# Weight rounding in a fused attention and feed-forward kernel: where a row's two words are added

## The chip, the cores and the metric

The kernel runs on one core of one Trainium2 chip. The metric is the device time of one execution in microseconds (us). The core has five engines, each with its own in-order instruction queue: PE (TensorE, the matrix products), DVE (VectorE), ACT (ScalarE), POOL (GpSimd) and SP (which here only issues transfers). They wait for each other through semaphores.

## The reference

Two blocks follow each other. The first is attention on q, k and v of shape (8, 12, 448, 64): q and k are normalised by their root mean square and a gain, then softmax(q k^T / 8) v. Its result, laid out as 3584 rows of 768, goes through a feed-forward layer:

```
def _moe_ref(x, w_in, w_out):
    h = x @ w_in            # 768 -> 2048
    r = np.maximum(h, 0.0)
    g = r * r
    return (g @ w_out).astype(np.float32)   # 2048 -> 768
```

q, k and v are 32-bit floats. The two weights come out of the set-up as 64-bit floats, since a 32-bit array is multiplied there by a 64-bit scalar. The kernel therefore reads each weight as two 32-bit words, a low and a high one that lie side by side, and makes a 32-bit float of them itself.

## The kernel before, in words

The work has these stages. The attention of the first two batch elements runs alone (`attention_alone`, twelve pairs of heads, about the first 133 us). Then comes the first product of the feed-forward layer for these (`first_product`, to about 262 us). From there on, the second product of one span of two batch elements is interleaved with the attention of the next, and so on through four spans; nothing of the change lies there.

Both products use a seven-product form of block multiplication. For it each weight is cut into blocks A11, A12, A21, A22 of 128 partitions by 384 words, and four sums of them are formed, S1 to S4. The seven operands A11, S2, S1, S3, A12, A22, S4 are stored to DRAM scratch (`w1s` for w_in, `w2s` for w_out) and read back in pieces (`sw`) as PE needs them, five pieces ahead.

The rounding is `prepare(t)`. There are 32 rows of 768 weights (`NFC` is 16, rows 0 to 15 belong to w_in, 16 to 31 to w_out), and each tick t has four quarters, between which the generator yields. An outer loop draws quarters: 48 of the first 52 over the attention alone, the others over the first product. The schedule is manual: on each engine the instructions stand in the order in which the program emits them. The steps of a row n are:

- `unsigned` (L578, ACT): the high words without sign, into an exponent buffer `eu`, one of four.
- L591 (DVE): clamps it. L596 (DVE): shifts it left by three; the result goes in place during the attention, and into a PSUM bank named `bits` from early in the first product on.
- L594 (ACT): scales the low words and makes integers of them.
- L601 (DVE): joins the sign bits of the high words to the shifted bits, into `eu`.
- `value` (L566, POOL), one tick later: the integer sum of low words and `eu` is the rounded weight. It is made in two instructions of 384 words, one for each block that the row fills. A row of w_in fills A11 and A12, or A21 and A22; a row of w_out A11 and A21, or A12 and A22.
- `total` (L572, POOL), after an odd row: S1, S2, S3, S4 of the pair of rows.
- the store of the seven blocks (L586, SP), three ticks after the odd row.

A pair of rows shares one of two block buffers in the tile `gC`, each of eight places: the seven operands in the order of the store, and A21 in place 7, which isn't stored. A new pair may be written into a buffer only once the store that reads it has landed. The words buffers, seven in turn, lie in `gC`, `gT` and a pool (`words`).

Other lines that are spoken of. In `attention_alone`, POOL takes the power -1/2 of a pair's mean squares (L702) and multiplies q by it (L704), behind the row sums (L699) and L700 on DVE; PE then transposes that pair (L742, tile `pt`), two pairs after its squares were taken. L767, L825 and L850 are PE's scores, values and sums of a pair; L784 on DVE adds up probabilities; L863 to L874 on DVE finish a pair, and L884 to L889 form sums of x for the first product. In `first_product`, seven products of 2.25 us (L1039, into banks `pa`, `pb`, `pc`, `pd`) make up one f of eight; DVE reads the banks: z (L1046), y (L1049), then g22, g21 and g12 (L1054), and ACT and POOL take it from there. pb, pc and pd share two banks in turn.

Of the kernel before, what the change touches and what calls it, by code (L numbers as in the profile page):

```python
# [9 lines left out]
F32 = mybir.dt.float32  # L10
U32 = mybir.dt.uint32
AF = mybir.ActivationFunctionType
ALU = mybir.AluOpType
# [373 lines left out]
def attention_then_ffn_bounded(  # L387
# [35 lines left out]
    nc = tc.nc  # L423
# [8 lines left out]
    NFC = DFF // P  # L432
# [47 lines left out]
    I32 = mybir.dt.int32  # L480
# [3 lines left out]
    NW = NPAIR * P  # L484
    HW = HC * P
# [7 lines left out]
    A11, S2, S1, S3, A12, A22, S4 = range(7)  # L493
    A21 = 7
# [3 lines left out]
    def pairs_of(words):  # L498
        both = words.rearrange("p (n two) -> p n two", two=2)
        return both[:, :, 0], both[:, :, 1]  # L500

    def words_of(n):
        place = n % WORDS
        if place == 0:
            at = BLOCKS * 8 * HW + EXPS * NW
            flat = stage[:, at:at + 2 * NW]
        elif place < 3:
            f = (NFC, HF)[place - 1] - 2
            flat = gT[:, f:f + 2, :].rearrange("p f n -> p (f n)")[:, 0:2 * NW]
        else:  # L510
            if (n, "words") not in spare:
                spare[n, "words"] = spare["pool"].tile([P, 2 * NW], F32, tag="words", name="words", bufs=WORDS - 3)
            flat = spare[n, "words"]
        return flat.bitcast(U32)

    def blocks_of(n):
        at = n // 2 % BLOCKS * 8 * HW
        return stage[:, at:at + 8 * HW].rearrange("p (k m) -> p k m", k=8)

    def exponents_of(n):  # L520
        at = BLOCKS * 8 * HW + n % EXPS * NW
        return stage[:, at:at + NW]
# [17 lines left out]
    def load_words(t, done):  # L540

        while loaded[0] <= t + WORDS - 3 and loaded[0] < max(done, 0) + WORDS:
            load_w(loaded[0])
            loaded[0] += 1

    def prepare(t):

        def there(n):  # L550
            return 0 <= n < 2 * NFC

        def parts(n):
            low, high = pairs_of(words_of(n))
            return exponents_of(n), exponents_of(n).bitcast(U32), low, high

        def value(n, half):
            if not there(n):
                return

            to = ((A11, A12), (A21, A22)) if n < NFC else ((A11, A21), (A12, A22))
            dst = blocks_of(n)[:, to[n % 2][half]]
            part = slice(half * HW, (half + 1) * HW)
            if doubles:
                _, eu, low, _ = parts(n)
                nc.gpsimd.tensor_tensor(*[x.bitcast(I32) for x in (dst, low[:, part], eu[:, part])], ALU.add)  # L566
            else:
                nc.gpsimd.tensor_copy(dst, words_of(n).bitcast(F32)[:, part])

        def total(n, dst, x, y, op):  # L570
            if there(n) and n % 2:
                nc.gpsimd.tensor_tensor(*[blocks_of(n)[:, i] for i in (dst, x, y)], op)  # L572

        def unsigned(n):

            if there(n) and doubles:
                e, _, _, high = parts(n)
                nc.scalar.activation(e, high.bitcast(F32), AF.Abs)  # L578

        if t == 0:  # L580
            unsigned(0)
        n = t - 3
        if there(n) and n % 2:
            c = n % NFC // 2
            dst = w1s[c] if n < NFC else w2s[:, c // 4, :, c % 4]
            nc.sync.dma_start(dst.rearrange("k p m -> p k m"), blocks_of(n)[:, 0:7])  # L586
            written[0] = n + 1
        if there(t) and doubles:
            e, eu, low, high = parts(t)

            nc.vector.tensor_scalar(e, e, 2.0 ** -15, 1.875 * 2.0 ** 16, ALU.max, ALU.min)  # L591
        yield
        if there(t) and doubles:
            nc.scalar.activation(low.bitcast(I32), low, AF.Copy, scale=2.0 ** -29)  # L594
            bits = banks.get("bits", eu)
            nc.vector.tensor_scalar(bits, eu, 3, 0x3FFFFFF8, ALU.logical_shift_left, ALU.bitwise_and)  # L596
        if t < 3:
            load_words(t, t - 1)
        yield
        if there(t) and doubles:  # L600
            nc.vector.scalar_tensor_tensor(eu, high, 0xC0000000, bits, ALU.bitwise_and, ALU.bitwise_or)  # L601
        total(t - 2, S3, A11, A21, ALU.subtract)
        total(t - 2, S4, A12, S2, ALU.subtract)
        value(t - 1, 0)
        yield
        unsigned(t + 1)
        value(t - 1, 1)
        total(t - 1, S1, A21, A22, ALU.add)
        total(t - 1, S2, S1, A11, ALU.subtract)
        load_words(t, t - 1)  # L610
        yield

    def ticks():
        for t in range(2 * NFC + 3):
            yield from prepare(t)
# [568 lines left out]
def kernel(  # L1184
# [50 lines left out]
    with tc.If(bits <= limit) as small_scores:  # L1235
        with tc.manual_schedule():
            attention_then_ffn_bounded(tc, *args, held)
# [32 lines left out]
```

## Time and profile before

| what | value |
|---|---|
| median of three runs | 1368.19 us (1366.46 to 1371.15) |
| profiled execution | 1369.76 us |
| its span, first to last instruction | 1367.8 us |
| granted TensorE clock in it | 0.998 |
| L566 on POOL | 64 instructions, 1.01 us each at the shortest |
| L572 on POOL | 64 instructions, 73.2 us |
| L601 on DVE | 32 instructions, 0.95 us each at the shortest |
| stores of a pair's blocks (L586) | 16, 1344 KB each, 5.7 to 10.3 us from issue to landing |

The profile's page gives the busy time of each engine and its share of the span, and the busy tenths of each engine in forty equal slices of 34 us. Groups name line, engine, operation, tiles (out<-in), shapes and count, then busy time and the mean of one in ns, then the idle time of the engine just before them with what ended it. An entry of the waits names who waited, then for whom. Busy time of PE overstates its work, since matrix products are pipelined; the idle time before its instructions is the better view of what it loses.

### The profile page before, as it was taken

The page shows a single profiled execution, that of the slowest core. Times are in us where ns is not written, and L with a number is a line of the kernel's source. Part 1 is how long each engine was busy: PE and PEld are TensorE (multiplying, and loading weights), DVE is VectorE, ACT ScalarE, POOL GpSimd, SP SyncE. Part 2 cuts the span into 40 slices and gives each one's busy share as a digit, 9 for nine tenths or more (in the row PEclk, how much of TensorE's full clock was granted, in tenths as well). Part 3 has the DMA queues.
Part 4 walks back from the last instruction along what each step waited for, and adds up shares of the span by engine and source line. Part 5 has one row for each costly group of instructions (what it writes and reads, how often), then busy time and mean ns, then how long its engine had stood idle before and what let it go on. Part 6 is the DMA issues. An engine that isn't in the chain of part 4 may idle for free.

```text
span 1367.8 us, 16894 instructions
## 1 busy us (share of the span) xinstructions
PE 1341.9 (98%) x5602; PEld 638.1 (47%) x5602; DVE 811.9 (59%) x1434; ACT 426.8 (31%) x657; POOL 633.2 (46%) x505
## 2 busy tenths in 40 slices
PE   8989999999999999999999999999999999999997
PEld 3333454444444455444444455444444445554553
DVE  6989776499986334467778523467788533332111
ACT  7875565433332011233332011233433101110000
POOL 6998887455563122555564122545666312220000
PEclk9999999999999999999999999999999999999999
DMA  9787998655675333446676433345765433333443
GB/s 245 194 234 198 329 390 291 184 117 118 133 141 126 97 86 87 102 113 136 130 140 121 111 93 87 100 110 106 157 124 114 99 91 89 90 90 101 106 114 66
DMA packets 434021, 190.12 MB, mean 139 GB/s; under 512 B 282885, under 2 KB 430725, under 8 KB 433925
## 3 DMA queue, kind: packets, MB, share of 16 engines
q1 hardware_dynamic: 425476, 180.10, 52.2%
q0 software_dynamic: 4736, 8.40, 2.4%
q8 instruction: 47, 0.77, 0.2%
q10 hardware_dynamic: 3712, 0.46, 0.2%
q14 instruction: 50, 0.40, 0.1%
HBM read 155.72 MB, written 33.16 MB: 138 GB/s over the span
## 4 chain that ended last, share of the span: by engine, by line
PE 86%; POOL 6%; DVE 4%; DMA 2%; issue 2%; ACT 1%; DVEq 0%; POOLq 0%; ACTq 0%
PE ps L1086 35%; PE pa L1039 10%; PE pd L1039 10%; PE pc L1039 10%; PE sc L759 7%; PE pav L836 6%; PE pb L1039 5%; POOL rstd L702 2%; POOL gC L566 1%; POOL gC L572 1%; DMA xT<-factors 1%; POOL qk L704 1%; DMA sw<-w1s 1%; ACT gT L771 0%; PE tot L850 0%
## 5 line engine op out<-in xcount | busy, mean ns | idle before, releaser
L1086 PE MATMUL ps<-gT,sw 128*128 128x448 f32 x768 | 301.1, 545 | 4.7 <-DVE p L1105 4.0
L1016 POOL TENSOR_TENSOR gT<-gT 128x448 f32<-128x448 f32 x96 | 93.9, 980 | 290.6 <-ACT gT L1012 290.6
L1086 PE MATMUL ps<-gC,sw 128*128 128x448 f32 x576 | 225.2, 542 | 0.0
L1086 PEld LDWEIGHTS ps<-gT,sw 128*128 128x128 f32 x768 | 144.4, 191 | 156.3 <-issue 145.6
L724 POOL TENSOR_TENSOR half<-half,mhalf 128x28 f32<-128x28 f32 x36 | 174.5, 4847 | 75.3 <-DVE half L723 72.1
L1086 PEld LDWEIGHTS ps<-gC,sw 128*128 128x128 f32 x576 | 108.0, 190 | 113.0 <-issue 110.1
L1039 PE MATMUL pa<-xT,sw 128*128 128x448 f32 x384 | 154.9, 539 | 0.0
L1012 ACT ACTIVATE gT<-gT 128x448 f32<-128x448 f32 x96 | 55.4, 577 | 311.6 <-DVE gT L1054 311.5
L761 ACT ACTIVATE pr<-sc 128x896 f32<-128x896 f32 x87 | 77.4, 915 | 121.5 <-PE sc L759 121.5
L759 PE MATMUL sc<-qkT 64*64 64x448 f32 (+1 forms) x1152 | 109.7, 496 | 0.0
L1039 PEld LDWEIGHTS pa<-xT,sw 128*128 128x128 f32 x384 | 72.9, 190 | 71.7 <-issue 70.3
L804 POOL DMA_DIRECT2D xT<-factors x72 | 38.0, 532 | 90.1 <-DMA factors<-square 61.0
L1054 DVE TENSOR_TENSOR gT<-z,pd 128x448 f32<-128x448 f32 x32 | 19.8, 620 | 99.7 <-PE pd L1039 99.6
L1039 PE MATMUL pb<-xC,sw 128*128 128x448 f32 x192 | 77.6, 540 | 1.4 <-issue 1.4
L1039 PE MATMUL pc<-xT,sw 128*128 128x448 f32 x192 | 77.5, 540 | 0.5 <-DMA sw<-w1s 0.5
L1039 PE MATMUL pd<-xT,sw 128*128 128x448 f32 x192 | 77.8, 541 | 0.0
L1039 PE MATMUL pc<-xC,sw 128*128 128x448 f32 x192 | 77.5, 540 | 0.0
L1039 PE MATMUL pd<-xC,sw 128*128 128x448 f32 x192 | 77.4, 539 | 0.0
L726 POOL TENSOR_TENSOR qk<-qk,half 128x448 f32<-128x448 f32 x72 | 75.0, 1061 | 2.8
L572 POOL TENSOR_TENSOR gC<-gC 128x384 f32<-128x384 f32 x64 | 73.2, 1162 | 2.5
L836 PE MATMUL pav<-pr,vt 64*64 64x448 f32 x348 | 72.7, 537 | 1.5 <-DVE half L872 1.5
L836 PE MATMUL rest<-pr,vt 64*64 64x448 f32 x348 | 72.7, 537 | 0.0
(135 smaller groups left out, 1879.7 us busy)
## 6 DMA issues: line engine op xcount, KB each, us to landing
sw<-w1s SPq DMA_DIRECT2D x224, 192.0 KB, 2.4
sw<-w2s SPq DMA_DIRECT2D x168, 256.0 KB, 3.2
w1s<-gC SPq DMA_DIRECT2D x8, 1344.0 KB, 7.5
w2s<-gC SPq DMA_DIRECT2D x8, 1344.0 KB, 8.1
out_dram<-osb SPq DMA_DIRECT2D x184, 56.0 KB, 1.9
qk<-in_q_dram SPq DMA_DIRECT2D x144, 56.0 KB, 3.6
qk<-in_k_dram SPq DMA_DIRECT2D x144, 56.0 KB, 2.9
xT<-factors POOLq DMA_DIRECT2D x72, 112.0 KB, 3.4
```

The lines of the kernel that those rows point to most:

```text
L572: nc.gpsimd.tensor_tensor(*[blocks_of(n)[:, i] for i in (dst, x, y)], op)
L702: nc.gpsimd.tensor_tensor(flat, flat, mhalf[:SP, 0:4 * NJ], ALU.pow)
L724: nc.gpsimd.tensor_tensor(half, half, mhalf, ALU.pow)
L726: nc.gpsimd.tensor_tensor(qkn[:, s], raw[:, s], half[:, s * NG:(s + 1) * NG].rearrange("p g -> p g ()").to_broadcast([P, NG, 32]), ALU.mult)
L759: nc.tensor.matmul(sc[part, h, 0:n], qkT[rows, 0, 1, keys], qkT[rows, 0, 0, of], start=True, stop=True)
L761: nc.scalar.activation(pr, sc[:, :, 0:n], AF.Exp)
L804: nc.gpsimd.dma_start(xT[h * D:(h + 1) * D, b % 2, hp], sums["out"][i % 2].rearrange("(h g) t -> h () (g t)", h=2)[h].to_broadcast([D, S]))
L836: nc.tensor.matmul(into, vs[i][rows, h, c, :], probs[i, c][rows, h, :], start=(c == 0), stop=(c == NF), skip_group_check=True)
L1012: nc.scalar.activation(g, src, AF.Relu)
L1016: nc.gpsimd.tensor_tensor(g, g, g, ALU.mult)
L1039: nc.tensor.matmul(ps, stream[n + i][:, c], rhs[:, c], start=first and c == 0, stop=c == HC - 1, skip_group_check=not first)
L1086: nc.tensor.matmul(ps, stream[n][:, c % 4], rhs_of[i][:, c], start=c == 0, stop=c == HF - 1)
```

## The change

The two POOL instructions of `value` become one DVE instruction for the whole row of 768 words. So that one access pattern can name the row's two blocks in rising order, a new function `place_of` puts the blocks of w_in rows at other places of the buffer: A21 at 0 and the seven operands at 1 to 7. The blocks of w_out rows stay where they were. The sums and the store use the same function. The call stands where that of the first half stood, behind L601 of the following row; the call of the second half, in the last quarter of the tick, goes. The branch for 32-bit weights is not taken here.

```diff
+    def place_of(n, k):
+
+        return 7 * int(n >= NFC) if k == A21 else k + int(n < NFC)
...
-        def value(n, half):
+        def value(n):
             if not there(n):
                 return
 
             to = ((A11, A12), (A21, A22)) if n < NFC else ((A11, A21), (A12, A22))
-            dst = blocks_of(n)[:, to[n % 2][half]]
-            part = slice(half * HW, (half + 1) * HW)
+            a, b = (place_of(n, k) for k in to[n % 2])
+            dst = blocks_of(n)[:, a:b + 1:b - a]
             if doubles:
                 _, eu, low, _ = parts(n)
-                nc.gpsimd.tensor_tensor(*[x.bitcast(I32) for x in (dst, low[:, part], eu[:, part])], ALU.add)
+                low, eu = (x.rearrange("p (h m) -> p h m", h=2) for x in (low, eu))
+                nc.vector.tensor_tensor(*[x.bitcast(I32) for x in (dst, low, eu)], ALU.add)
...
         def total(n, dst, x, y, op):
             if there(n) and n % 2:
-                nc.gpsimd.tensor_tensor(*[blocks_of(n)[:, i] for i in (dst, x, y)], op)
+                nc.gpsimd.tensor_tensor(*[blocks_of(n)[:, place_of(n, i)] for i in (dst, x, y)], op)
...
-            nc.sync.dma_start(dst.rearrange("k p m -> p k m"), blocks_of(n)[:, 0:7])
+            first = place_of(n, A11)
+            nc.sync.dma_start(dst.rearrange("k p m -> p k m"), blocks_of(n)[:, first:first + 7])
...
         total(t - 2, S3, A11, A21, ALU.subtract)
         total(t - 2, S4, A12, S2, ALU.subtract)
-        value(t - 1, 0)
+        value(t - 1)
         yield
         unsigned(t + 1)
-        value(t - 1, 1)
         total(t - 1, S1, A21, A22, ALU.add)
         total(t - 1, S2, S1, A11, ALU.subtract)
```

More of the change, by code (lines that the diff above doesn't have):

```diff
@@ L561, in value @@
             to = ((A11, A12), (A21, A22)) if n < NFC else ((A11, A21), (A12, A22))
-            dst = blocks_of(n)[:, to[n % 2][half]]
-            part = slice(half * HW, (half + 1) * HW)
+            a, b = (place_of(n, k) for k in to[n % 2])
+            dst = blocks_of(n)[:, a:b + 1:b - a]
             if doubles:
                 _, eu, low, _ = parts(n)
-                nc.gpsimd.tensor_tensor(*[x.bitcast(I32) for x in (dst, low[:, part], eu[:, part])], ALU.add)
+                low, eu = (x.rearrange("p (h m) -> p h m", h=2) for x in (low, eu))
+                nc.vector.tensor_tensor(*[x.bitcast(I32) for x in (dst, low, eu)], ALU.add)
             else:
-                nc.gpsimd.tensor_copy(dst, words_of(n).bitcast(F32)[:, part])
+                nc.vector.tensor_copy(dst, words_of(n).bitcast(F32)[:, 0:NW].rearrange("p (h m) -> p h m", h=2))
         def total(n, dst, x, y, op):
             if there(n) and n % 2:
-                nc.gpsimd.tensor_tensor(*[blocks_of(n)[:, i] for i in (dst, x, y)], op)
+                nc.gpsimd.tensor_tensor(*[blocks_of(n)[:, place_of(n, i)] for i in (dst, x, y)], op)
         def unsigned(n):
```

## The prediction

> **What bounds the kernel now.** I read the page's busy shares and slices first, then stretches of the attention stage, then waits and groups there, then the timelines of single rows.
>
> ```profile
> PE 1341.9 (98%) x5602; PEld 638.1 (47%) x5602; DVE 811.9 (59%) x1434; ACT 426.8 (31%) x657; POOL 633.2 (46%) x505
> DVE  6989776499986334467778523467788533332111
> POOL 6998887455563122555564122545666312220000
> ```
>
> TensorE (PE) is never long without work, so a change elsewhere gains at most what PE loses where the change acts. The edited rows run from about 28 to 246 us. There VectorE (DVE) and GpSimd (POOL) are both near nine tenths in the first four slices, the attention alone. The stretches of that time, whose columns are length, then busy time and count of PE, PEld, DVE, ACT and POOL:
>
> ```profile
> 60.00:113.00 53.00, 48.56 (x252) 18.83 (x252) 45.46 (x59) 41.07 (x67) 52.14 (x35) 1.00 0.83 229
> 113.00:137.00 24.00, 21.50 (x103) 7.84 (x100) 22.42 (x33) 11.12 (x19) 19.49 (x13) 1.00 0.84 207
> 137.00:262.00 125.00, 124.47 (x330) 62.02 (x329) 81.00 (x108) 70.22 (x109) 95.75 (x89) 1.00 0.90 315
> ```
>
> From 60 to 113 us POOL never rests (52.1 of 53.0) and PE loses 4.4 us; from 113 to 137 PE loses 2.5; in the first product (137 to 262) it loses 0.5. Who ended PE's waits, between 20 and 135 us (us in total, times, longest):
>
> ```profile
> PEld pt L742 <- POOL qk L704: 9.4, 6, 3.0
> PE pt L742 <- POOL qk L704: 4.6, 5, 2.2
> PE tot L850 <- DVE gT L863: 0.8, 1, 0.8
> ```
>
> PE waits for POOL's product q times rstd (L704) before it can transpose the next pair. POOL does it in order, behind this, in the groups of 20 to 135 us:
>
> ```profile
> L702 POOL TENSOR_TENSOR rstd<-rstd,mhalf 112x16 f32<-112x16 f32 x9 | 28.4, 3159 | 5.1 <-DVE rstd L700 4.9
> L572 POOL TENSOR_TENSOR gC<-gC 128x384 f32<-128x384 f32 x20 | 26.7, 1348 | 0.8
> L566 POOL TENSOR_TENSOR gC<-gT,gC 128x384 int32<-128x384 int32 x8 | 12.3, 1558 | 0.0
> L566 POOL TENSOR_TENSOR gC<-words,gC 128x384 int32<-128x384 int32 x10 | 12.0, 1218 | 0.0
> ```
>
> L566, with a third group of 4 (6.3 us), is 30.6 us: 27% of POOL there, and it is what goes.
>
> [...] The two timelines agree (start, length):
>
> ```profile
> 93.85 0.55 DVE L591 TENSOR_SCALAR gC<-gC 128x768 f32<-128x768 f32 x1
> 94.43 1.26 DVE L596 TENSOR_SCALAR gC<-gC 128x768 uint32<-128x768 uint32 x1
> 95.72 1.67 DVE L601 SCALAR_TENSOR_TENSOR gC<-gT,gC 128x768 uint32<-128x768 uint32 x1
> ...
> 93.82 2.75 POOL L566 TENSOR_TENSOR gC<-gC 128x384 int32<-128x384 int32 x2
> ```
>
> L596 takes 0.55 us elsewhere and 1.26 beside L566, and two L566 take 2.75 in place of 2.03: each side waits for the other's instruction to end. [...]
>
> **The change part by part.** In the built program 64 POOL instructions go and 32 come on VectorE, each right behind a row's L601 and working on the row before. Other engines keep their order; only waits change owner. The added one is no ordinary addition: it is built over 1,536 16-bit halves.
>
> Its price. VectorE's groups from 137 to 262 us:
>
> ```profile
> L601 DVE SCALAR_TENSOR_TENSOR gC<-words,bits 128x768 uint32<-128x768 uint32 x9 | 8.6, 951 | 0.2
> L1054 DVE TENSOR_TENSOR gT<-z,pd 128x448 f32<-128x448 f32 x8 | 4.9, 617 | 6.4 <-PE pd L1039 6.2
> ```
>
> Two halves a cycle make it 768 steps: 0.95 us like L601, which reads its words at the same stride. One half a cycle: the slope is (951-617)/320 = 1.04 ns an element, so 951 + 768 x 1.04 = 1.75 us. I take 1.05: pairs, with a tenth for reads and writes that no row shows. Both ends stay for the range.
>
> 1. Attention to 113 us. Rows 0 to 9 are added there, four before 60 us and six after: +4.2 and +6.3 us of VectorE. Off comes its waiting for L566: each VectorE instruction that starts while L566 runs, less the shortest of its form in the timeline, makes 4.0 and 2.5 us. Net +0.2 before 60 us, where VectorE is busy 38.4 of 40.0, and +3.8 after, where it has 7.5 idle. POOL loses 12 L566, 15.3 us with their waits, of its 52.1. The 5.6 us from the row sums (L699) to L704 then run without a queue: L699 began at 71.5, which gives 77.1 where PE wanted it at 79.9. I let PE gain 4.2 of the 4.4.
>
> 2. The tail, 113 to 137 us. VectorE is a chain without gaps there (0.9 idle, waiting for PE) into PE's first pb product. Two additions, +2.1; off comes 3.6 of waiting for L566. Gain 1.5, of which 0.8 is taken, since VectorE may arrive later out of step 1.
>
> 3. The first product, 137 to 262 us. 20 additions, +21 us, less 4.8 of waiting: VectorE goes from 81 to 97 of 125. Idle time is no full cover here. The PSUM bank that z (L1046), g22 and g12 (L1054) read is wanted again one product (2.25 us) later; where VectorE reads at once, 1.4 us are left, so an addition in front fits. Where it is late already, it doesn't:
>
> ```profile
> 186.32 0.96 DVE L596 TENSOR_SCALAR bits<-gC 128x768 uint32<-128x768 uint32 x1
> 187.31 0.95 DVE L601 SCALAR_TENSOR_TENSOR gC<-gC,bits 128x768 uint32<-128x768 uint32 x1
> 188.18 0.61 DVE L1046 TENSOR_TENSOR z<-p,pb 128x448 f32<-128x448 f32 x1
> ```
>
> Its product ended at 187.05 and PE took the bank again at 189.14: 0.34 is left, so 1.05 in front of it stalls PE 0.7. Going through the 24 reads so, I find that, about 0.3 at three g12, and nothing elsewhere: loss 1.5 us.
>
> 4. Waits that move. The addition of an even row waits until the store of its block pair has landed; POOL had this (3.5 us in four waits), now VectorE stands, with PSUM reads queued behind it and PE behind those. Stores landed 1.5 to 3.6 us before L601's end, so 0, at worst 1 us for two rows. The POOL sums (L572) start later, since an odd row's addition stands behind the next row's L601: up to 3.4 us, of which the store on SP has 1.2 to 3.8 to spare. Behind it on SP are sw loads, with five buffers of 2.25 us against 2.4 to landing: 0. ACT's waits for POOL become waits for VectorE a tick old: 0.
>
> Sum: -4.2 - 0.8 + 1.5 = -3.5 us. The profiled execution took 1369.76 us (span 1367.8 and 2.0 around it), 1.6 above the median of 1368.19; -3.5 on the median is **1364.7**.
>
> **The rivals.** (a) As worked out, 1361.3 to 1367.5: with all 6.9 of PE's idle gained and no loss it would be 1361.3. (b) VectorE takes POOL's place as the bound. Before 60 us it is at 96%, and steps 1 and 2 rest on its idle time; if contention with L572 and L704, which stay, costs the additions 0.3 each (3.6), or PE's tighter pace exposes its waits for ACT, the 5 us are gone: 1367 to 1370. Against it: 2.8 us of slack between L704 and PE. (c) Slower: the addition takes one half a cycle, 1.75 us. In steps 1 and 2 that is 8.4 us more VectorE, which eats the gain; in step 3 it exceeds the 1.4 us that a punctual PSUM read has, so that some ten of the reads stall PE 0.4 to 1 us: about +6, 1374. It decides from about 1.4 us on. [...] That the change doesn't do what it says can be left out: the program has the 32 instructions.
>
> **How the numbers follow.** A measurement of this kernel can tell about 0.3%, 4.1 us, from no change: faster means below 1364.1. (a) 0.60, its centre just above that line: 0.32 below, 0.28 within. (b) 0.20: 0.17 within, 0.03 slower. (c) 0.20: 0.18 slower, 0.02 within. Faster 0.32, same 0.47, slower 0.21. Range 1360.5 to 1373.0: (a) and (b) whole, and the near part of (c); the far part is left out.
>
> **What would show it.** Right: the new VectorE group near 1.05 us x32; POOL in 60 to 113 us far under full; PE's wait for L704 gone; L596 and L601 at their shortest more often; PE idle of 1 to 2 us in the first product, ended by VectorE's z or gT. Wrong: a mean of 1.4 or more for the addition; PE in the attention still waiting for L704, with POOL now waiting for L700; PE idle over 3 us in the first product; the addition waiting for stores.

## The result, and the profile after

The changed kernel took 1365.05 us (median of 12 runs, 1362.23 to 1367.43), the kernel before 1368.58 (12 runs): 3.5 us less in the medians, and a ratio of 0.9970, 95% interval 0.9962 to 0.9978, which is -4.1 us. A repeat gave 1365.61 against 1368.12, ratio 0.9977 (0.9970 to 0.9984), -3.1 us. So the kernel is faster by about 0.3%. The profiled execution of the first comparison took 1364.95 us, span 1363.0.

The lines of the changed kernel stand five or six further down: the addition is L571, the sums L577 (L572 before), the store L592, the steps of a row L597, L602 and L607 (L591, L596, L601), POOL's power and product L707 and L709 (L702, L704), the first product L1044 and z L1051 (L1039, L1046).

The page after, first the busy times, then the slices of VectorE and GpSimd:

```profile
PE 1340.7 (98%) x5602; PEld 637.6 (47%) x5602; DVE 826.5 (61%) x1466; ACT 426.7 (31%) x657; POOL 570.0 (42%) x441
...
DVE  6999788599987333467778523557788633332111
...
POOL 5786334456573122655564222545566312220000
```

VectorE has 32 instructions and 14.6 us more, POOL 64 and 63.2 us less. The three groups of the addition, between 20 and 262 us (count, busy us, mean ns, idle time before):

```profile
L571 DVE CUSTOM_DVE_ANT_0 gC<-words,gC 128x1536 uint16<-128x1536 uint16 x17 | 18.0, 1057 | 0.1
...
L571 DVE CUSTOM_DVE_ANT_0 gC<-gT,gC 128x1536 uint16<-128x1536 uint16 x10 | 9.9, 988 | 0.0
...
L571 DVE CUSTOM_DVE_ANT_0 gC<-gC 128x1536 uint16<-128x1536 uint16 x5 | 4.7, 947 | 0.0
```

They sum to 32.6 us, 1.02 each on average and 0.94 at the shortest. VectorE's busy time grew by 18.0 less than that, but not all of it is waiting for L566 that went: of VectorE's other instructions, those up to 262 us are 11.2 us shorter in sum (11.2 to 13.3 in three pairs of traces), those in the unedited code behind it 2.7 us in this pair, and the rest is overlap of neighbours by about 0.1 us. The same stretches as before (length, then busy time and count of PE, PEld, DVE, ACT, POOL):

```profile
60.00:113.00 53.00, 50.08 (x260) 19.20 (x260) 50.35 (x63) 42.35 (x70) 45.40 (x25) 1.00 0.87 242
113.00:137.00 24.00, 21.55 (x103) 7.88 (x100) 23.32 (x38) 11.05 (x19) 16.25 (x8) 1.00 0.76 183
137.00:262.00 125.00, 122.97 (x327) 61.73 (x326) 94.90 (x128) 69.02 (x108) 49.84 (x44) 1.00 0.90 314
```

From 60 to 113 us PE still loses 2.9 us, where it lost 4.4; in the tail 2.4 as before; in the first product 2.0 in place of 0.5. VectorE is now the fullest engine beside PE up to 137 us. PE's waits from 18 to 137 us in the changed kernel (us in total, times, longest):

```profile
PE pav L830 <- DMA vt<-in_v_dram: 1.5, 1, 1.5
PE pt L747 <- POOL qk L709: 1.5, 1, 1.5
...
PE tot L855 <- DVE gT L868: 1.0, 1, 1.0
```

Five waits of PE for POOL's q times rstd (L709, before L704), 4.6 us, have become one of 1.5; a wait for the transfer of v is new. In the second trace of this kernel these two are one wait of 2.5 us for L709 and none for v; in the third they are 1.5 and 1.4.

**Where a trace loses time.** To compare traces step by step, I took each of PE's 5602 matrix products in its order (it is the same in all kernels here; the first one into bank `pb`, near 137 us, ends the attention) and, for each, the shortest time from its start to the next start over the thirteen traces of this study. What a trace takes above that is its loss. A part of it needs a word. In some places PE runs at half its clock for a few microseconds, as in the second trace of the kernel before:

```profile
95.40:98.60 3.20, 3.20 (x10) 0.85 (x8) 2.05 (x2) 3.14 (x6) 3.04 (x3) 0.50 1.17 265
```

The number behind the five engines' entries is the granted clock, 0.50. These spells are counted apart, since the same program has them in one trace and not in the next; how much of a loss is the spell's is an estimate. In us:

| trace | to the first pb | first product | after 262 us | half-clock spells |
|---|---|---|---|---|
| before, three traces | 9.03, 9.28, 9.08 | 1.50, 1.81, 1.29 | 8.80, 5.56, 6.22 | 1.49, 1.53, 0 |
| after, three traces | 7.37, 7.62, 7.31 | 2.84, 2.85, 3.25 | 4.48, 5.74, 4.53 | 1.49, 1.10, 2.73 |
| attention rows alone | 8.58 | 1.29 | 7.59 | 1.54 |
| product rows alone | 9.14 | 4.00 | 8.10 | 4.16 |
| additions of rows 4 to 31 left out | 2.43 | 1.10 | 8.65 | 1.54 |
| additions made twice | 15.12 | 18.86 | 5.17 | 6.46 |
| addition in the last quarter | 7.39 | 2.16 | 4.19 | 2.97 |
| store issued by POOL | 11.48 | 4.84 | 5.49 | 2.32 |
| last quarter and later stores | 7.08 | 0.60 | 5.16 | 1.45 |

The first two columns repeat within 0.3 and 0.5 us for one program, so they can be read as effects of it. The last two cannot from one trace.

### The profile page after: what moved, and what is told of

The parts are those of the page before. It is cut to its first block, busy times and chain, and to the rows that moved or that the text cites. A ratio compares the mean times of both kernels' runs of the same rounds, so it can differ in the third digit from the quotient of the medians.

```text
span 1363.0 us, 16832 instructions
## 1 busy us (share of the span) xinstructions
PE 1340.7 (98%) x5602; PEld 637.6 (47%) x5602; DVE 826.5 (61%) x1466; ACT 426.7 (31%) x657; POOL 570.0 (42%) x441
## 4 chain that ended last, share of the span: by engine, by line
PE 87%; DVE 7%; POOL 2%; issue 2%; ACT 1%; DMA 0%; DVEq 0%; ACTq 0%; POOLq 0%
PE ps L1091 36%; PE pd L1044 10%; PE pa L1044 10%; PE pc L1044 10%; PE sc L764 7%; PE pav L841 7%; PE pb L1044 5%; PE sc L772 1%; POOL rstd L707 1%; DVE gC L571 1%; PE tot L855 1%; DVE gC L607 1%; PE pav L830 1%; DVE gT L789 1%; DVE gC L597 0%
## 5 line engine op out<-in xcount | busy, mean ns | idle before, releaser
L1044 PE MATMUL pa<-xT,sw 128*128 128x448 f32 x384 | 154.9, 539 | 0.0
L577 POOL TENSOR_TENSOR gC<-gC 128x384 f32<-128x384 f32 x64 | 78.7, 1247 | 67.5 <-DVE gC L571 66.2
L1044 PEld LDWEIGHTS pa<-xT,sw 128*128 128x128 f32 x384 | 72.9, 190 | 71.7 <-issue 70.4
L1044 PE MATMUL pb<-xC,sw 128*128 128x448 f32 x192 | 77.6, 540 | 2.1 <-issue 1.5
L1044 PE MATMUL pd<-xT,sw 128*128 128x448 f32 x192 | 77.9, 542 | 1.3 <-DVE z L1051 1.3
L1044 PE MATMUL pc<-xC,sw 128*128 128x448 f32 x192 | 77.4, 539 | 0.0
L1044 PE MATMUL pd<-xC,sw 128*128 128x448 f32 x192 | 77.4, 539 | 0.0
L1044 PE MATMUL pc<-xT,sw 128*128 128x448 f32 x192 | 77.4, 539 | 0.0
```

The lines of the kernel that those rows point to most:

```text
L577: nc.gpsimd.tensor_tensor(*[blocks_of(n)[:, place_of(n, i)] for i in (dst, x, y)], op)
L1044: nc.tensor.matmul(ps, stream[n + i][:, c], rhs[:, c], start=first and c == 0, stop=c == HC - 1, skip_group_check=not first)
```

## The experiments

**Halves of the change.** The rows added during the attention (0 to 11) and those added during the first product (12 to 31), each moved alone. The other rows keep the two POOL instructions of 384 words, issued where the kernel before issues them; all rows have the new places in the buffer.

```diff
+        def on_pool(n):
+            return n >= 12          # the other half: n < 12
...
         def value(n):
-            if not there(n):
+            if not there(n) or on_pool(n):
...
+        value_half(t - 1, 0)        # POOL, third quarter
...
+        value_half(t - 1, 1)        # POOL, last quarter
```

The attention rows alone:

> Rows 0 to 11 (added during the attention alone) are added on VectorE as after the change, rows 12 to 31 in two POOL operations as before it. Theory A, the prediction's steps: the attention rows give 5.0 us and the product rows cost nothing here, so 5.0 us less than before, about 1363.5, and 1.5 less than the changed kernel. Theory B, read from the changed kernel's trace: the attention gives only some 2 us, what is left of the 3.5 us arises after 262 us in waits that vary from run to run; then about 2 us less than before, with the first product as dense as before (PE idle under 1 us from 137 to 262). Theory C, VectorE took POOL's place as the bound: no change to before.

Measured: 1366.02 us, ratio 0.9978 (0.9968 to 0.9988), -3.0 us. Up to the first pb it loses 8.58, of which 1.2 comes from a longer start at 18.9 us, before the first addition of this kind; without that it is 7.4, as after. The first product loses 1.29, as before.

The product rows alone:

> The other half: rows 0 to 11 in two POOL operations as before, rows 12 to 31 on VectorE as after. Theory A: 1.5 us more than before, and 6.5 more than rows 0 to 11 alone on VectorE. Theory B: the trace shows PE losing 1.3 to 1.9 us more in the first product, so 1 to 2 us more than before. Theory C says the same for these rows. In all, the attention keeps its waits of PE for L709 (4 to 5 us of PE idle) as before.

Measured: 1370.98 us, ratio 1.0012 (1.0002 to 1.0022), +1.7 us. The attention is that of the kernel before (9.14), the first product loses 4.00, 2.5 more than before. So the two halves have the signs that the steps gave them: the attention gains, the first product pays. Their sum, -1.3 us, is less than the whole change's, but each has an interval of about 1.4 us to either side. This half also has the new places of the blocks, and its attention loses as much as before, so it is not the places that gain there.

**Without the additions.** The additions of rows 4 to 31 are left out, so these weights are not the rounded ones; rows 0 to 3 are added as in the change. It gives about the most that a cheaper addition could bring.

```diff
-            if not there(n):
+            if not there(n) or n >= 4:
```

> The integer additions of rows 4 to 31 are left out on both engines (the blocks keep what rows 0 to 3 left there), so that POOL is relieved and VectorE pays nothing. Theory A: PE's idle time of 6.9 us before 262 us goes but for the first 60 us, and no stall in the first product: 6 to 7 us less than before, 1362. Theory B: about 3 us less than before, since PE then meets other waits (transfers of v, ACT) in the attention. Theory C: as A, 6 to 7 less, with the changed kernel's missing 3 us lying in VectorE's additions.

Measured: 1361.93 us, ratio 0.9940 (0.9922 to 0.9957), -8.2 us. The attention loses 2.43, the product 1.10. PE's waits from 18 to 137 us in this kernel hold what is left of the two that the changed one has:

```profile
PE pav L830 <- DMA vt<-in_v_dram: 0.3, 1, 0.3
...
PE pt L747 <- POOL qk L709: 0.2, 1, 0.2
```

So both come from the additions being on VectorE, and 28 of them cost the changed kernel about 5 us in the attention and 1.9 in the first product, against an ideal that has them nowhere.

**Twice.** Each VectorE addition is made a second time, into the same place.

```diff
                 nc.vector.tensor_tensor(*[x.bitcast(I32) for x in (dst, low, eu)], ALU.add)
+                nc.vector.tensor_tensor(*[x.bitcast(I32) for x in (dst, low, eu)], ALU.add)
```

> Every addition on VectorE is made twice in a row, which doubles the 0.95 us that one takes: this is the price of rival (c). Theory A with the prediction's rival (c): about 6 us more than before, 1374.5, 9 to 10 more than the changed kernel; PE idle in the first product 5 us or more, ended by z (L1052) and gT (L1060). Theory B: the same in the first product, and in the attention less than 1 us, since VectorE still has idle time there: 4 to 5 more than the changed kernel. Theory C: VectorE bounds the attention, so every addition there adds its whole 0.95 us: 12 x 0.95 = 11 us there and 5 in the product, 16 more than the changed kernel.

Measured: 1396.47 us, ratio 1.0197 (1.0177 to 1.0217), +27 us over before and 31 over after. 32 additions of 0.95 us are 30.4 us: in all, the second one costs as much time as its full length. By the table 7.7 us of it are lost in the attention, 15.9 in the first product, and 4.7 are half-clock spells beyond those of the changed kernel. The stretches, in the order of columns given above:

```profile
60.00:113.00 53.00, 46.42 (x233) 17.70 (x232) 51.97 (x64) 39.17 (x65) 41.21 (x22) 0.97 0.73 205
...
137.00:262.00 125.00, 108.36 (x274) 50.42 (x275) 107.07 (x134) 57.32 (x89) 46.45 (x39) 0.96 0.80 270
```

VectorE is full from 60 to 113 us (51.97 of 53.0), and in the first product PE waits for its reads of the banks again and again (z and g, twelve waits, 12.8 us), though VectorE still has 18 us idle there. The cover that hides most of the first addition seems used up by it. None of the theories on record came near it.

**The addition in the last quarter of the tick,** away from L607.

```diff
-        value(t - 1)
         yield
         unsigned(t + 1)
+        value(t - 1)
```

> The whole change, with the addition of a row put in the last quarter of its tick, away from L607. In the first trace of the changed kernel POOL stood between 69 and 73 us behind five VectorE instructions without a gap (L602, L789, L607, the addition, L789), where L709 took 3.50 us in place of 1.04 and PE waited 1.46 us for it. Theory A (the length of such a train decides when POOL gets in): with one instruction less in it L709 takes under 2.5 us there and PE waits under 0.7 us, and the attention is about 0.8 us shorter; the stall near 190 us in the first product, which came from an addition in front of a late read, moves or goes, up to 1.2 us; in all 1 to 2 us faster than the changed kernel. Theory B (the amount of VectorE work decides, not its order): the stalls turn up elsewhere at the same sum, and the time is that of the changed kernel within 0.7 us.

Why it was tried shows in two timelines of the changed kernel around PE's wait at 71 us, POOL first, then VectorE (start, length, instruction):

```profile
64.36 5.08 POOL L707 TENSOR_TENSOR rstd<-rstd,mhalf 112x16 f32<-112x16 f32 x1 [0.55 <-DVE rstd L705]
69.52 3.50 POOL L709 TENSOR_TENSOR qk<-qk,rstd 112x512 f32<-112x512 f32 x1
...
75.90 3.14 POOL L707 TENSOR_TENSOR rstd<-rstd,mhalf 112x16 f32<-112x16 f32 x1
```

```profile
68.84 0.55 DVE L602 TENSOR_SCALAR gC<-gC 128x768 uint32<-128x768 uint32 x1
69.30 1.08 DVE L789 TENSOR_TENSOR gT<-gT 112x896 f32<-112x896 f32 x1
70.30 0.96 DVE L607 SCALAR_TENSOR_TENSOR gC<-words,gC 128x768 uint32<-128x768 uint32 x1
71.17 0.95 DVE L571 CUSTOM_DVE_ANT_0 gC<-words,gC 128x1536 uint16<-128x1536 uint16 x1
72.04 1.93 DVE L789 TENSOR_TENSOR gT<-gT 112x896 f32<-112x896 f32 x1
```

L709 takes 1.04 us where nothing holds it. Here it took 3.50: by these times, it began at 69.5, stood through L789, L607 and the addition, which follow each other without a gap, and ran after them, while the second L789 waited for it (1.93 in place of 1.08). L707 before it took 5.08 in place of 3.14. So POOL did not get its turn after one instruction of VectorE here, but after three; what the two engines share is not in the trace.

Measured: 1365.16 us, ratio 0.9978 (0.9969 to 0.9987); the changed kernel beside it on the same chip took 1365.61. L709 took 2.64 us there, and PE waited 0.7 for it; the stall near 190 us in the first product went, and the product loses 2.16. That is close to what theory A said of each place (under 2.5 and under 0.7 for L709). But PE waited 0.6 for L709 elsewhere in the attention, the wait near 87 us, where v is late, stayed (1.5), that for L868 in the tail was 1.8 in place of 1.0, and the two times are the same within their intervals: theory B for the sum.

**The store issued by POOL,** behind its own last sum, in place of SP.

```diff
-            nc.sync.dma_start(dst.rearrange("k p m -> p k m"), blocks_of(n)[:, first:first + 7])
+            nc.gpsimd.dma_start(dst.rearrange("k p m -> p k m"), blocks_of(n)[:, first:first + 7])
```

> The whole change, with the store of a block pair issued by POOL, which makes the last of its sums (L577), in place of SP. In the first trace of the changed kernel SP stood from 63.9 to 75.8 us for the store of the first pair, v of the next heads stood behind it, landed near 88.4 and PE waited 1.5 us for it. Theory A (the store is what holds SP, and the freed POOL has room): PE's wait for v goes, 1.5 us less in the attention; POOL pays for 16 issues, perhaps 0.5 to 1 us each, which the attention's 7.6 us of idle POOL time from 60 to 113 us hide; 1 to 1.5 us faster than the changed kernel. Theory B (v is late because its place or the queues are late, not SP): PE's wait for v stays near 1.5 us, and the issues on POOL delay L707 and L709: 0 to 3 us slower.

Measured: 1373.1 us, ratio 1.0041 (1.0030 to 1.0053): 7.5 slower than the changed kernel. The wait for v went. But SP was not free at once: with no store in front of it, the load of q stood until L709 had ended. POOL's line is from its timeline, the other from SP's:

```profile
71.88 3.51 POOL L709 TENSOR_TENSOR qk<-qk,rstd 112x512 f32<-112x512 f32 x1
```

```profile
75.42 0.31 SPq L315 DMA_DIRECT2D qk<-in_q_dram  x1
```

So the store is not alone in holding SP; the starved L709 does it too, because it reads what the load of q will overwrite. With the issues, 0.94 to 1.15 us each on POOL (the expectation's 0.5 to 1 us was an estimate; POOL's issues of `xT`, L804 in the kernel before, took 0.52 to 0.56), PE waited 4.0 us for L709 in three waits, in place of 1.5 in one, and 2.3 us for a stored block in the first product; 1.1 us of its loss in the attention stands before the first store, at 19 us.

**Last quarter and later stores.** As the last-quarter kernel, and the stores of rows 0 to 7 half a tick later on SP.

```diff
-        n = t - 3                          # store, first quarter
-        if there(n) and n % 2:
+        store(True)                        # first quarter: rows from 8 on
...
+        store(False)                       # third quarter: rows 0 to 7
         total(t - 2, S3, A11, A21, ALU.subtract)
```

> The whole change with the addition in the last quarter of its tick, and with the stores of the first four block pairs (rows 0 to 7) asked for half a tick later on SP, so that the loads of two attention steps, v among them, no longer stand behind a store that waits for L577. With the addition in the last quarter alone PE still waited 1.6 us near 87 us for v. Theory A (v is late only because SP stood in front of a store): that wait goes, the attention is 1.5 us shorter, and the time is 1 to 1.5 us under that of the last-quarter kernel, about 1363.8. Theory B (the attention's pace is set elsewhere, so that one wait is followed by another): the wait goes, another of about 1 us takes its place, and the time is that of the last-quarter kernel within 0.7 us. If the addition now waits for a store in place of that, slower by 1 us or more.

Measured: 1364.96 us, ratio 0.9976 (0.9966 to 0.9986), in a later comparison than the last-quarter kernel's; the two ratios are the same within their intervals. The edit missed its aim: on SP no load stood between the old and the new place of the first store, which still held SP for 10.7 us, until L577 ended at 74.2; PE waited 1.4 us for v. Only the second store was passed by a load of v. This kernel's first product lost 0.60 in its trace, less than before; its edit does not touch those rows, so it is probably a matter of where the stretch fell against PE's reads, not a merit of the later store.

**More traces of the two kernels.**

> The kernel before, unchanged, for a second trace of it: how far two traces of one program differ stretch by stretch. Theory A (my steps account for the gain): the two traces of before agree to 0.5 us at the start of pb and at 262 us once spells of PE at half its clock are taken off, and the rest of the span differs by less than 1.5 us. Theory B (most of the measured 3.5 us arises after 262 us in waits that vary from run to run): the part after 262 us differs by 2 us or more between the two, and the first trace, with three long waits there, was a long one.

> The changed kernel, unchanged, for a second trace and a firmer ratio. In the first pair of traces, spells of half clock taken off, the changed kernel was 1.85 us ahead at the start of pb, 0.5 ahead at 262 us, and 6 ahead at the end. Theory A: the two stalls of 1.5 us in the attention (71 us, PE waits for L709; 87 us, PE waits for the transfer of v) and the 1.4 us stall near 190 us in the first product are there again, so that they belong to the program, and the ratio is 0.997 again. Theory B: the part after 262 us gains under 2 us against the second trace of before, and the ratio is nearer 0.999.

> A third trace of the kernel before. In the first two, PE lost the same 9.0 and 9.4 us to waits up to the end of the attention and 1.5 and 1.8 us in the first product, but 9.8 and 5.1 us after 262 us. Theory A (the gain sits in the edited stretch): the third trace loses the same there within 0.5 us, spells of half clock left out. Theory B (the rest of the span, and the spells of half clock that follow a long wait of PE, vary from run to run by more than the change): the part after 262 us lies anywhere from 4 to 10 us, and a spell follows one of PE's waits of 2 us or more near 91, 307, 452 or 1097 us.

> A third trace of the changed kernel. In the first two, spells of half clock left out, PE lost 7.2 us and 7.9 to waits up to the end of the attention, 2.8 and 2.8 in the first product and 4.0 and 5.3 after 262 us. Theory A (the gain sits in the edited stretch): the third trace loses 1 to 2 us less than before in the attention and 1.0 to 1.3 more in the first product, within 0.5. Theory B (the rest varies by more than the change): after 262 us it lies anywhere from 4 to 10 us.

Measured: before again 1367.69 us, ratio 1.0000 (0.9989 to 1.0010); the ratio of after again is given above. The third traces came with one time each, 1365.28 (before) and 1366.60 (after), which says nothing about the two. The traces are the first two rows of the table. The losses of the edited stretch repeat, as theory A says, though not wait by wait: the changed kernel's wait for v is absent from its second trace. After 262 us the three traces of before differ by 3.2 us without the spells, 4.7 with them, as theory B says. The first trace of before was a long one: two waits of 2.0 us of PE for VectorE, near 452 and 1097 us, and a spell behind the second.

## Why the forecast was right, and where its sum was not

The number was right: 1364.7 forecast, 1365.05 and 1365.61 measured. The working was right in its direction for each half, but the gain that it put in the attention was sized at about twice what came. So the number came out by luck for the most part: some 3 of the 3.5 us arise where the forecast expected nothing. The interval of the ratio, 0.08% to either side, is also finer than the 0.3% that a measurement was said to tell.

- **The price.** 1.05 us was taken, 1.02 measured; at the shortest two halves take the time of one word in L607 (0.94 and 0.95), so rival (c) at 1.75 us is out. No trace of the kernel before decided between 0.95 and 1.75; that it would be pairs was the author's estimate, and so was the tenth put on top. The waiting that comes off VectorE was put at 4.0 + 2.5 + 3.6 + 4.8 = 14.9 us; its other instructions up to 262 us became 11.2 to 13.3 us shorter.
- **Step 1, the attention to 113 us.** 4.2 us was taken. At the product near 113.7 us the changed kernel is 2.0 us ahead over three traces, spells left out. The failing term is "the 5.6 us from the row sums (L699) to L704 then run without a queue". For six of nine pairs they did: L709 ended 4.55 to 4.57 us behind the row sums. For the fifth pair it took 8.95, since VectorE's run of instructions without a gap kept POOL out (L707 5.08 us, L709 3.50). PE's wait for this product was to go; it fell from 4.6 to 1.5 us (2.5 and 1.5 in the other traces); POOL was still busy 45.4 of 53.0 us, and from 20 to 135 us it now stood 19.6 us for VectorE in front of the power (4.9 before), which had been named as a sign of being wrong. This is rival (b)'s contention, turned round: the additions cost POOL (that L709 2.5 us) more than POOL the additions (0.08 us each, the mean of 1.02 less the shortest). And the queue on SP was worked out for the sw loads alone; in the attention the loads of q, k and v stand behind the store, or behind L709, and v was 1.5 and 1.4 us late in two of three traces.
- **Step 2, the tail.** A gain of 0.8 was taken, and 0.4 was lost: VectorE is busy 23.3 of 24.0 us there, 0.9 more than before, and PE's wait for its L868 grew from 0.8 to 1.0, 1.6 and 1.1 in the three traces.
- **Step 3, the first product.** A loss of 1.5 was taken; it is 2.98 - 1.53 = 1.45 over three traces. The place was named too: the read of z near 188 us. Its lines after:

```profile
188.60 0.95 DVE L607 SCALAR_TENSOR_TENSOR gC<-gC,bits 128x768 uint32<-128x768 uint32 x1
...
189.47 0.95 DVE L571 CUSTOM_DVE_ANT_0 gC<-words,gC 128x1536 uint16<-128x1536 uint16 x1
...
190.34 0.61 DVE L1051 TENSOR_TENSOR z<-p,pb 128x448 f32<-128x448 f32 x1
...
191.01 1.40 PE L1044 MATMUL pd<-xT,sw 128*128 128x448 f32 x3 [1.35 <-DVE z L1051]
```

  PE stood 1.35 where 0.7 was worked out, and up to 0.7 at a g12 where 0.3 was.
- **Step 4, moved waits.** 0 was taken. No addition waited for a store. The POOL sums start later, as said; what that did to SP in the attention is counted in step 1.
- **The sum.** In the edited stretch the change nets -1.7 + 1.45, about -0.25 us, not -3.5. This rests on what is set down to the spells: counted at 1.7 us for each 3.41 us of half clock it is -0.6, and with the spells left in the changed kernel reaches 262 us 1.0 us later in the mean of three traces (four spells up to there against one). The times say -3.1 to -4.1. One further piece repeats: near 309 us PE waits 1.5 us in each trace of before, and 0, 0.8 and 0.7 in those of after. In before, an addition of VectorE (L782) and a product of POOL (L726), each in two halves, start together and seem to take turns: the two halves of L782 take 2.69 us, where one is 0.62 at the shortest, and those of L726 2.22, where one is 0.93. In after POOL starts its product at 307.96 and VectorE gets its two halves through in 1.27. Before, then after:

```profile
305.94 2.22 POOL L726 TENSOR_TENSOR qk<-qk,half 128x448 f32<-128x448 f32 x2
```

```profile
305.95 2.69 DVE L782 TENSOR_TENSOR acc<-acc,half 64x448 f32<-64x448 f32 x2
```

```profile
307.13 1.27 DVE L787 TENSOR_TENSOR acc<-acc,half 64x448 f32<-64x448 f32 x2
```

  That is unedited code, and neither half of the change alone has the gain (PE waits 1.6 us there in both), so it is probably a matter of when the two meet, not of a load taken off. It is worth about 1 us. The other 2 us of the measured gain could not be placed. Three traces of each differ by 1.3 us in the mean of their spans (1365.3 against 1364.0), and one trace of a program differs from the next by up to 4.6; the two waits near 452 and 1097 us and the spells hold most of that. Whether the change shortens them on average stays open.
- **The rivals.** (c)'s size was far off. It put +6 us on an addition of 1.75 us. At about 1.9 us, the doubled addition, it is +27. It counted only the reads of the banks that came late by themselves and let idle time of VectorE take the rest; but once several reads are late, each seems to delay what stands behind it, which is read from the sum and was not shown wait by wait. Its deciding point was put at 1.4 us and was not measured; between 0.95 and 1.9 us the cost passes from about 7 us, against no addition at all, to 7 + 31.

## What to carry to other kernels

When work moves between two engines that lengthen each other's instructions in the trace, as VectorE and POOL do here, look at the longest run of instructions without a gap on the new engine and at what the old one must still do in that time: the old engine lost 63.2 us of load here and then waited its turn (L709 3.50 us in place of 1.04). Idle time of the receiving engine was cover only as far as each of its urgent reads had slack; the first addition here cost about a quarter of its length (6.9 of 26.6 us for 28 rows, by the table), the second all of it (31 of 30.4 us by the times, the half-clock spells included). And a forecast that comes out right is no proof of its sum: split both traces at the edges of the edited code, and take a second and third trace before a wait far from the edit is put down to it.

## What was not expected of the hardware

- POOL can be held through several VectorE instructions, three near 70 us in the first trace of the changed kernel. A product of 1.04 us took 3.50 and 4.51 us in the first two traces of the changed kernel and 2.64 in the last-quarter kernel, a power of 3.14 up to 5.10.
- A wait of PE costs more than its length in some executions. The granted clock on record has 19 spells of half clock (0.50) in the thirteen traces, the one at the end of each span left out: 17 last 3.41 us, two 6.83, and by estimate, half of the length, 3.41 us at half clock put off about 1.7 us of work. Within a trace they begin whole multiples of 3.41 us apart: in the first trace of before, the one near 1099 us and the one at the end are 266.24 us apart, 78 times 3.413, and in the first of after, those near 22 us and at the end 1338.03, 392 times. Cut into stretches of 3.41 us on that beat, the thirteen traces have 16 stretches in which PE is busy 0.34 to 1.48 us, and each has half clock behind it (in these two traces, 1.45 us busy from 1096.0 and 1.48 from 19.0); of all the others, with more, five have. So in these traces a spell goes with where a wait falls on the beat. The wait of 2.2 us near 91 us lies in one stretch in the second trace of before (PE busy 1.30 us of it, a spell behind it); in the other two it is divided over two stretches (busy about 2.6 and 2.0 us, 2.5 and 2.1), and no spell follows. Why the clock falls is not in the traces.
